# Three blocks instead of two by halves of the weights at the start of a fused attention and two-MLP kernel

## The chip, the cores and the metric

The kernel runs on one core of a Trainium2 chip. The metric is the device time of one execution in microseconds (us), the median of several runs. A profiled execution has its own time, and the span from its first to its last instruction is a little shorter than that.

The core has five engines that run side by side and wait for each other through semaphores: TensorE (PE; its weight loads are listed as PEld), VectorE (DVE), ScalarE (ACT), GpSimd (POOL) and SyncE (SP), which here issues all DMA transfers. The 128-partition on-chip memory is SBUF; matmul results land in PSUM, in eight banks of 128 x 512 f32.

## The reference

Windowed causal attention (window 128, with a linear bias per head), then two MLPs one after the other, on 4 x 576 = 2304 tokens, 8 heads of 64:

```python
scores = scale * np.matmul(q, k.transpose(0, 1, 3, 2))
bias = slopes[:, None, None] * (-np.abs(rel).astype(np.float32))[None, :, :]
mask = (rel >= 0) & (rel < window)
scores = np.where(mask, scores + bias[None], -1000000000.0)
attn = np.exp(scores - np.max(scores, axis=-1, keepdims=True))
attn = attn / (np.sum(attn, axis=-1, keepdims=True) + 1e-09)
x = np.matmul(attn, v)                       # (2304, 512) after the transpose
h = x @ w_in                                 # 512 -> 2048
x = np.where(h >= 1, h, np.where(h <= -1, 0.0, (h + 1) ** 2 / 4)) @ w_out
h2 = x @ w_in2
out = (h2 * np.clip(h2 + 3.0, 0.0, 6.0) / 6.0) @ w_out2
```

The weights arrive as 64-bit floats and are converted on the chip. Products are made from a high and a low part of each factor, three matmuls for one.

## The kernel before, in words

**Attention in ticks.** The tokens are cut into 11 units (lines 72 to 80): 256, 320 | 192, 256, 128 | 256, 128, 192 | 192, 256, 128 tokens. Each unit has 8 heads, each head one step per 128 queries, so the units have 16, 24, 16, 16, 8, 16, 8, 16, 16, 16, 8 steps (`unit_steps`, line 242), 160 in all. `Attention.tick` (lines 513 to 527) is a software pipeline: tick t does stage A (scores, mask, exponential) of step t, stage B (transposes of the probabilities through bank `t`, `th` and `tl` out of it) of step t - 2, and stages C (times v, into bank `r`) and D (into x) of steps three or four back. It also prepares one head ahead (`prep`: the high and low parts of k, q and v) and loads two heads beyond that one. So a unit's x is complete `LAG_D` = 4 ticks after its last step began. Heads of units 0 to 2 are "whole": they normalise after the product with v, stage A issues filler matmuls for them (`keep_busy`, line 345), and v is split only from unit 3 on (line 308). Bank `t` alternates with `t2` up to unit 3 and is alone from unit 4 on (line 373); `s` and `r` are single.

**Weights in 16 pairs.** Pair f holds 128 columns of w_in and 128 rows of w_out. `W1.load` issues one 512 KB DMA; `conv_tick` (lines 199 to 210) converts: two ScalarE passes for pair n, and three VectorE passes, a ScalarE copy and a VectorE subtraction for pair n - 1 (lines 178, 179, 185 to 189, 137, 144).

**The first MLP in blocks and chunks.** `blocks1` cuts the tokens into three blocks of 256 (the x of block j comes from unit j) and four of 384. `chunks.run` does one chunk: `first` for pair f (12 matmuls into bank `h0` or `h1`, line 549; then r, g on VectorE, ScalarE and POOL, lines 578 to 582), then `flush`, the `second` of the pair two chunks back (12 matmuls into the accumulators, line 591). Around it the hook is called twice, between and after; these are the slots. `run_block` runs a block over A (pairs 0 to 7), Z (8 to 15) or FULL. A block run by halves writes its sums to HBM after A (`finish`, line 617); in Z they are read back two chunks before the end (`fetch`, line 604) and added (line 614) instead of copied.

**The order around the change** is written by hand in lines 779 to 788: after 20 ticks ahead of all chunks, `spread(part, ticks, conv)` hands out so many ticks and conversions evenly over the slots of a pass, the ticks over all but the last two slots, and one `W1.load` per slot while there are any. It traces them in this order: block 0 A with 24 ticks and 8 conversion calls, block 1 A with 10 and 4, block 0 Z with 6 and what is left (3), block 1 Z with 4, block 2 FULL with 20, then the blocks of 384. SyncE runs its DMAs in exactly the order written (line 720). The other engines are ordered by the planner, which starts from this order and moves an instruction ahead of another where it expects the other to wait.

The x of all blocks lies in one SBUF tile; block 3's x overwrites that of block 0 and of half of block 1, block 4's that of block 2 and the other half of block 1 (`x_base`, lines 90 to 97).

Of the kernel before, what the change touches and what calls it, by code (L numbers as in the profile page):

```python
# [32 lines left out]
LAG_B, LAG_C, LAG_C_SPLIT, LAG_D = 2, 3, 4, 4  # L33
# [5 lines left out]
def tile_window_attention_two_mlps(  # L39
# [16 lines left out]
    B, H, D, S = qT.shape  # L56
# [3 lines left out]
    KF = DFF // P  # L60
# [9 lines left out]
    blocks1 = [(a, N1) for a in range(0, 3 * N1, N1)] + [(a, WIDE) for a in range(3 * N1, NT, WIDE)]  # L70
# [12 lines left out]
    needs = [min(i + 1 for i, (a, n) in enumerate(units) if a + n >= t0 + m) for t0, m in blocks1]  # L83
    assert needs[:3] == [1, 2, 3]
    first_wide = 3
# [26 lines left out]
    def keep_busy(bank, n):  # L112


        for a in range(0, n, 2 * P):
            nc.tensor.matmul(bank[:, a:a + 2 * P], zeros[:, :P], zeros, start=True, stop=True, skip_group_check=True)

    def make_consts():
        rel = cpool.tile([P, 2, PIECE], F32, tag="m", name="rel")[:, 0, :2 * P]


        nc.gpsimd.iota(rel, pattern=[[1, 2 * P]], base=-P, channel_multiplier=-1,
                       allow_small_or_imprecise_dtypes=True)
        nc.gpsimd.affine_select(out=rel, in_=rel, compare_op=ALU.is_ge, fill=NEG / min(slopes),
                                base=P, pattern=[[-1, 2 * P]], channel_multiplier=1)
        last = nc.gpsimd.affine_select(out=rel, in_=rel, compare_op=ALU.is_ge, fill=NEG / min(slopes),
                                       base=WINDOW - 1 - P, pattern=[[1, 2 * P]], channel_multiplier=-1)
        with tc.issue_after(last.ins):
            make_identity(nc, ident)
        nc.vector.tensor_copy(dist, rel)  # L130
# [93 lines left out]
    heads = []  # L224
# [17 lines left out]
    unit_steps = [sum(1 for n, _ in steps if heads[n].unit == j) for j in range(len(units))]  # L242
# [484 lines left out]
    A, Z = range(KF // 2), range(KF // 2, KF)  # L727

    def run_block(mlp1, j, part, hook):
        for f in part:  # L730
            chunks.run(mlp1, j, f, part, j, lambda: hook(f, 0), lambda: hook(f, 1))

    with ExitStack() as actx:
        mlp1 = Mlp1(W1, blocks1, rpool, gpool)
        raw = actx.enter_context(tc.tile_pool(name="raw", bufs=2))
        proc = actx.enter_context(tc.tile_pool(name="proc", bufs=2))
        work = actx.enter_context(tc.tile_pool(name="work", bufs=2))
        dist = actx.enter_context(tc.tile_pool(name="dist", bufs=1)).tile([P, 2 * P], BF16, tag="dist", name="dist")
        zeros = actx.enter_context(tc.tile_pool(name="zeros", bufs=1)).tile([P, 2 * P], BF16, tag="zeros", name="zeros")
        att = Attention(raw, proc, work, XX)  # L740

        nc.vector.memset(zeros, 0.0)

        nc.scalar.copy(zeros[:, 0:1], nc.const_aps.tensor(0.0, [P, 1], F32))
        bank = psum.tile([P, BANK], F32, tag="h1", name="busy")
        for _ in range(WARM_UP):
            keep_busy(bank, BANK)
        make_consts()
        for vt in att.vts:
            nc.gpsimd.memset(vt[:, :, 0:2 * D + 2:2 * D + 1], 1.0)  # L750
        att.more_loads(1)
        W1.load()

        n_pre = unit_steps[0] + LAG_D
        for t in range(n_pre):
            att.tick()
            if t % 3 == 0:
                W1.load()
            if t >= n_pre - 2:
                W1.conv_tick()  # L760

        def spread(part, ticks, conv):

            slots = 2 * len(part)
            att0, conv0 = att.t, W1.n_conv

            def hook(f, after):
                k = 2 * (f - part[0]) + after + 1
                W1.load()
                while W1.n_conv < conv0 + min(conv, -(-conv * k // slots)) and W1.conv_tick():  # L770
                    pass
                while att.t < att0 + min(ticks, -(-ticks * k // (slots - 2))):
                    att.tick()

            return hook

        run_block(mlp1, 0, A, spread(A, unit_steps[1], KF // 2))
        run_block(mlp1, 1, A, spread(A, 10, KF // 4))  # L780
        run_block(mlp1, 0, Z, spread(Z, unit_steps[2] - 10, KF // 2))
        run_block(mlp1, 1, Z, spread(Z, 4, KF))
        for j in range(2, len(blocks1) - 1):
            if j == first_wide:

                mlp1.tags = ("h0",)
            ticks = sum(unit_steps[:needs[j + 1]]) + LAG_D - att.t
            run_block(mlp1, j, FULL, spread(FULL, max(0, ticks), 0))
# [100 lines left out]
```

## Time and profile before

| | us |
|---|---|
| median of 3 runs | 1000.5 |
| lowest, highest | 999.63, 1001.77 |
| profiled execution | 999.68 |
| its span, first to last instruction | 997.9 |
| PE busy in the span | 968.9 (97%) |
| DVE busy | 602.9 (60%) |
| ACT busy | 515.9 (52%) |
| POOL busy | 259.3 (26%) |

A profile row of a timeline begins with the start and the length in us; `x12` is the number of instructions merged in it, and `[0.81 <-DVE ...]` says how long the engine stood idle before it and what ended the wait. Matmuls are pipelined: the length of one is longer than the distance to the next, so costs of TensorE are read from starts to starts. A window's row gives, for each engine, the busy time and the number of instructions.

### The profile page before, as it was taken

The numbers are of one execution on the slowest core, as the hardware profiler recorded it, in microseconds if no ns is written. First come the engines' busy times: TensorE is split into PE (matmuls) and PEld (weight loads), VectorE is DVE, ScalarE is ACT, GpSimd is POOL, SyncE is SP. The second block draws the span as 40 slices with busy tenths as digits, with TensorE's granted clock in tenths as the row PEclk, the third lists the DMA queues.
The fourth block names the chain that finished last, engine by engine and source line by source line (L and its number), as shares of the span: only waits on it lengthen the run. The fifth ranks groups of instructions, "written<-read, shape, count | busy, mean of one in ns | idle before, by whom it ended". The sixth has DMA issues, their size and how long they took to land.

```text
span 997.9 us, 16828 instructions
## 1 busy us (share of the span) xinstructions
PE 968.9 (97%) x5748; PEld 882.8 (88%) x5748; DVE 602.9 (60%) x1544; ACT 515.9 (52%) x1260; POOL 259.3 (26%) x403
## 2 busy tenths in 40 slices
PE   7799999999999999999999999999999999999998
PEld 5687888999999998899999999999988888888886
DVE  4889996587678666668764998942242224223222
ACT  5688874567657566656653878522242223222121
POOL 3335454456545555455530000000000000000000
PEclk9899999999999999999999999999999999999999
DMA  5685823223212121222203884000030002001001
GB/s 171 168 258 173 271 66 87 78 67 94 75 42 80 50 80 44 63 59 80 62 12 105 293 277 169 1 1 1 1 106 1 1 1 84 1 1 43 1 1 42
DMA packets 75092, 80.00 MB, mean 80 GB/s; under 512 B 8704, under 2 KB 67072, under 8 KB 75008
## 3 DMA queue, kind: packets, MB, share of 16 engines
q1 hardware_dynamic: 75008, 78.94, 25.8%
q8 instruction: 45, 0.74, 0.3%
q14 instruction: 39, 0.32, 0.1%
HBM read 68.42 MB, written 10.49 MB: 79 GB/s over the span
## 4 chain that ended last, share of the span: by engine, by line
PE 85%; DVE 6%; ACT 4%; issue 2%; DMA 2%; POOL 1%; SPq 0%; ACTq 0%; DVEq 0%; POOLq 0%
PE h L549 37%; PE acc L646 20%; PE acc L591 17%; PE s L329 3%; PE r L466 3%; PE r L411 2%; PE t L380 1%; PE t L381 1%; DVE kl L305 1%; DVE r L578 1%; DMA qr<-qT 1%; ACT p L353 1%; DVE r L580 1%; DVE p L350 1%; DMA vr<-v 1%
## 5 line engine op out<-in xcount | busy, mean ns | idle before, releaser
L549 PE MATMUL h<-x,wa 128*128 128x384 f32 (+1 forms) x1344 | 231.5, 316 | 4.4 <-DVE r L580 2.5
L591 PE MATMUL acc<-g,wa 128*128 128x384 f32 (+1 forms) x1344 | 228.8, 315 | 1.7 <-POOL g L144 1.5
L549 PEld LDWEIGHTS h<-x,wa 128*128 128x128 f32 x1344 | 207.6, 190 | 7.0 <-DVE r L580 4.4
L549 PE MATMUL h<-x,wb 128*128 128x512 f32 (+1 forms) x960 | 210.5, 368 | 0.0
L591 PEld LDWEIGHTS acc<-g,wa 128*128 128x128 f32 x1344 | 206.3, 189 | 4.0 <-POOL g L144 2.2
L646 PE MATMUL acc<-wb,g 128*128 128x512 f32 x864 | 209.4, 390 | 0.0
L549 PEld LDWEIGHTS h<-x,wb 128*128 128x128 f32 x960 | 176.3, 188 | 25.0
L646 PEld LDWEIGHTS acc<-wb,g 128*128 128x128 f32 x864 | 161.7, 188 | 32.3
L636 DVE SCALAR_TENSOR_TENSOR r<-r,h 128x512 f32<-128x512 f32 (+1 forms) x80 | 50.7, 633 | 195.5 <-ACT r L635 195.4
L635 ACT ACTIVATE r<-h 128x512 f32<-128x512 f32 (+1 forms) x80 | 44.4, 556 | 207.9 <-PE h L549 207.8
L137 ACT CAST g<-r 128x384 fp32r<-128x384 f32 (+2 forms) x192 | 98.3, 512 | 69.6 <-DVE r L636 48.7
L144 POOL TENSOR_TENSOR g<-r,g 128x256 fp32r<-128x256 f32 (+1 forms) x96 | 92.0, 958 | 129.2 <-ACT g L137 114.0
L579 ACT ACTIVATE r<-r 128x384 f32<-128x384 f32 (+1 forms) x112 | 53.6, 478 | 93.5 <-DVE r L578 93.3
L353 ACT ACTIVATE p<-p,sm 128x256 f32<-128x256 f32 (+2 forms) x160 | 76.0, 476 | 24.4 <-DVE sm L350 21.6
L144 DVE TENSOR_TENSOR g<-r,g 128x384 fp32r<-128x384 f32 (+1 forms) x96 | 59.9, 624 | 44.7 <-ACT g L137 44.6
L578 DVE TENSOR_SCALAR r<-h 128x384 f32<-128x384 f32 (+1 forms) x112 | 55.5, 496 | 37.4 <-PE h L549 33.2
L144 POOL TENSOR_TENSOR qs<-qr,qs 64x256 fp32r<-64x256 f32 (+3 forms) x88 | 68.8, 781 | 28.4 <-issue 7.5
L580 DVE TENSOR_TENSOR r<-h,r 128x384 f32<-128x384 f32 (+1 forms) x112 | 55.7, 497 | 28.9 <-ACT r L579 28.3
L350 DVE CUSTOM_DVE_ANT_0 p<-s,dist 128x256 f32<-128x256 f32 (+2 forms) x160 | 59.7, 375 | 11.1 <-PE s L329 8.8
L358 POOL TENSOR_SCALAR p<-p,sm 128x256 f32<-128x256 f32 (+1 forms) x104 | 48.1, 463 | 61.7 <-DVE sm L357 37.4
L329 PE MATMUL s<-kh,qs 128*128 128x256 f32 (+2 forms) x160 | 55.0, 347 | 1.8 <-POOL qs L144 1.2
L305 DVE SCALAR_TENSOR_TENSOR kl<-kr,kh 128x256 fp32r<-128x256 f32 (+4 forms) x88 | 51.7, 587 | 7.3 <-ACT kh L303 7.1
(75 smaller groups left out, 1153.5 us busy)
## 6 DMA issues: line engine op xcount, KB each, us to landing
rawa<-w_in SPq DMA_DIRECT2D x16, 512.0 KB, 5.6
rawa<-w_out SPq DMA_DIRECT2D x16, 512.0 KB, 5.1
rawb<-w_in SPq DMA_DIRECT2D x16, 512.0 KB, 3.8
rawb<-w_out SPq DMA_DIRECT2D x16, 512.0 KB, 4.6
kr<-kT SPq DMA_DIRECT2D x80, 64.0 KB, 2.3
out<-o SPq DMA_DIRECT2D x18, 256.0 KB, 2.1
qr<-qT SPq DMA_DIRECT2D x64, 64.0 KB, 2.3
vr<-v SPq DMA_DIRECT2D x24, 128.0 KB, 2.4
```

What stands on the lines that cost most here:

```text
L137: nc.scalar.copy(hi, x)
L144: engines[eng].tensor_tensor(out=lo, in0=x, in1=hi.bitcast(F32), op=ALU.subtract)
L305: nc.vector.scalar_tensor_tensor(out=u.kl[:, :nk], in0=u.kr[:, :nk], scalar=unit, in1=u.kh[:, :nk].bitcast(F32), op0=ALU.mult, op1=ALU.sub ...
L329: nc.tensor.matmul(ps[:m, :nk], q[:, qo:qo + m], k[:, ko:ko + nk], start=(w == 0), stop=(w == len(parts) - 1))
L350: nc.vector.tensor_tensor_reduce(out=pt[:m, :nk], in0=ps[:m, :nk], in1=dist[:m, bo:bo + nk], scale=-slopes[u.h], scalar=3.0e38, op0=ALU.ad ...
L353: nc.scalar.activation(out=pt[:m, :nk], in_=pt[:m, :nk], func=AF.Exp, bias=sm[:m, 0:1], scale=-1.0, accum_out=None if u.whole else sm[:m, ...
L549: nc.tensor.matmul(ps[:, :n], self.W.w_in(a, c, f), self.x_chunk(x, b, c, n), start=(k == 0), stop=(k == 3 * KC - 1))
L578: nc.vector.tensor_scalar(out=r[:, :n], in0=ps[:, :n], scalar1=-1.0, scalar2=1.0, op0=ALU.max, op1=ALU.min)
L579: nc.scalar.activation(out=r[:, :n], in_=r[:, :n], func=AF.Square, bias=0.5, scale=0.5)
L580: nc.vector.tensor_tensor(out=r[:, :n], in0=ps[:, :n], in1=r[:, :n], op=ALU.max)
L591: nc.tensor.matmul(acc[i][:, o * n:(o + 1) * n], self.W.w_out(a, f)[:, e * P:(e + 1) * P], g[:, b, :n], start=(first and k == 0 and o == 0 ...
L646: nc.tensor.matmul(acc[t][:, :DM], g[:, b, t * P:(t + 1) * P], self.W.w_out(a, f), start=(first and k == 0), stop=(last and k == 2))
```

## The change

The third block (block 2) joins the first two: its pass over the first half of the weights comes right after block 1's, and its pass over the second half after block 1's. For that, the attention of unit 2 has to be complete before the end of block 1's first pass, so that pass gets 16 ticks instead of 10. The conversions of the second half of the weights are spread over block 1 A (2 calls), block 2 A (3) and the first chunk of block 0 Z (the last 2). The remaining 24 ticks up to block 3, all of units 3 and later, are handed out 3, 8 and 13 to block 0 Z, block 1 Z and block 2 Z; the bounds 3 and 11 are where stage D begins to overwrite x that block 0, then block 1, still needs. Block 2 gets one more `finish` and one `fetch`. The number of matmuls, ticks, loads and conversions is unchanged.

```diff
+        t_end = sum(unit_steps[:3]) + LAG_D
+        per_chunk = 2 * len(heads[H * first_wide].qbs)
+        assert LAG_D == LAG_C_SPLIT and per_chunk == 4
         run_block(mlp1, 0, A, spread(A, unit_steps[1], KF // 2))
-        run_block(mlp1, 1, A, spread(A, 10, KF // 4))
-        run_block(mlp1, 0, Z, spread(Z, unit_steps[2] - 10, KF // 2))
-        run_block(mlp1, 1, Z, spread(Z, 4, KF))
-        for j in range(2, len(blocks1) - 1):
+        run_block(mlp1, 1, A, spread(A, t_end - att.t, KF // 8))
+        run_block(mlp1, 2, A, spread(A, 0, 3))
+        run_block(mlp1, 0, Z, spread(Z, per_chunk - 1, KF))
+        run_block(mlp1, 1, Z, spread(Z, 2 * per_chunk, 0))
+        assert att.t == t_end + 3 * per_chunk - 1
+        run_block(mlp1, 2, Z, spread(Z, sum(unit_steps[:needs[3]]) + LAG_D - att.t, 0))
+        for j in range(first_wide, len(blocks1) - 1):
```

## Rows read from the trace of the kernel before

**Rows 1.** The page, part 1: busy us, share of the span, instructions.
```profile
PE 968.9 (97%) x5748; PEld 882.8 (88%) x5748; DVE 602.9 (60%) x1544; ACT 515.9 (52%) x1260; POOL 259.3 (26%) x403
```

**Rows 2.** Windows by pass (A0, A1, Z0, Z1, B2): stretch, length, busy us of each engine.
```profile
29.24:98.33 69.09, 61.28 (x448) 52.28 (x446) 63.33 (x153) 56.16 (x129) 29.83 (x30) 0.98 0.66 198
98.33:135.40 37.07, 36.35 (x281) 32.37 (x280) 34.23 (x85) 31.38 (x74) 18.21 (x21) 1.00 0.64 206
135.40:167.77 32.37, 30.43 (x239) 27.93 (x238) 26.84 (x70) 19.09 (x53) 16.90 (x20) 1.00 0.35 101
167.77:193.86 26.09, 26.09 (x223) 26.09 (x221) 15.40 (x46) 12.61 (x35) 10.76 (x16) 1.00 0.24 74
193.86:257.90 64.04, 63.38 (x534) 62.37 (x532) 50.52 (x180) 44.45 (x144) 35.81 (x63) 1.00 0.27 71
```

**Rows 3.** Timeline of PE in Z1: start, length, instructions.
```profile
179.37 1.60 PE L591 MATMUL acc<-g,wa 128*128 128x256 f32 x12
180.81 0.22 PE L466 MATMUL r<-th,vs 128*128 128x128 f32 x1
...
181.46 1.61 PE L549 MATMUL h<-x,wa 128*128 128x256 f32 x12
```

**Rows 4.** Timeline of PE at the start of Z0, a tick of a whole head.
```profile
135.40 1.60 PE L549 MATMUL h<-x,wa 128*128 128x256 f32 x12
136.93 0.58 PE L411 MATMUL r<-vr,th 128*64 128x65 f32 x4
...
137.89 0.33 PE L591 MATMUL acc<-g,wa 128*128 128x256 f32 x1
```

**Rows 5.** Groups by shape: count, busy us, mean ns, idle before; conversion, x, add.
```profile
L189 DVE CUSTOM_DVE_ANT_0 ma<-rawa,ma 128x2048 uint16<-128x2048 uint16 x16 | 21.5, 1341 | 0.7 <-ACT rawa L179 0.6
...
L144 DVE TENSOR_TENSOR wa<-ma,wa 128x1024 fp32r<-128x1024 f32 x16 | 20.9, 1304 | 0.9 <-ACT wa L137 0.8
L187 DVE SCALAR_TENSOR_TENSOR ma<-rawa,ma 128x1024 uint32<-128x1024 uint32 x16 | 20.8, 1297 | 0.1
...
L185 DVE TENSOR_SCALAR ma<-ma 128x1024 uint32<-128x1024 uint32 x16 | 12.5, 780 | 0.9 <-ACT ma L178 0.8
...
L144 DVE TENSOR_TENSOR x<-xf,x 128x192 fp32r<-128x192 f32 x8 | 3.6, 446 | 0.0
...
L614 DVE TENSOR_TENSOR o<-acc,o 128x512 f32<-128x512 f32 x4 | 2.7, 686 | 0.2 <-PE acc L591 0.2
```

**Rows 6.** Waits of PE, 98 to 170 us: us in total, times, longest; first and last of five.
```profile
PE h L549 <- DVE sm L356: 0.8, 1, 0.8
...
PE t L381 <- ACT th L137: 0.2, 1, 0.2
```

**Rows 7.** Timeline in Z0 where unit 3's v is waited for: ScalarE and TensorE.
```profile
157.91 0.35 ACT L141 CAST vs<-vr 128x192 fp32r<-128x192 f32 x1 [1.32 <-DMA vr<-v]
...
159.65 1.57 PE L591 MATMUL acc<-g,wa 128*128 128x256 f32 x11 [0.64 <-POOL g L144]
```

**Rows 8.** Window in B2 that holds the eight ticks of unit 4.
```profile
219.60:244.40 24.80, 24.78 (x209) 24.25 (x208) 20.33 (x75) 18.46 (x61) 14.77 (x29) 1.00 0.34 86
```

**Rows 9.** Timelines of DVE, POOL and PE around a wait for bank `t` in block 4.
```profile
367.63 1.15 DVE L144 TENSOR_TENSOR x<-xf,x 128x192 fp32r<-128x192 f32 x1
368.70 0.21 DVE L393 TENSOR_TENSOR tl<-t,th 64x64 fp32r<-64x64 f32 x1
...
367.36 1.20 POOL L144 TENSOR_TENSOR g<-r,g 128x384 fp32r<-128x384 f32 x1 [0.46 <-ACT g L137]
...
369.06 0.30 PE L380 MATMUL t<-ident,p 128*128 128x128 f32 x1 [1.08 <-DVE sm L356]
```

**Rows 10.** Waits of PE for transposes in block 4, 342 to 448 us.
```profile
PE t L380 <- DVE sm L356: 2.4, 3, 1.1
PE t L381 <- DVE sm L356: 2.4, 4, 0.8
```

**Rows 11.** Tile kr, loads between 100 and 117 us, from issue to landing.
```profile
DMA to landing us min/median/max: 2.0/8.3/9.0
```

## The prediction

> **What bounds the kernel now.** I read the page first. TensorE is busy for 97% of the span [rows 1], so the change can only give back time in which TensorE waits, or lose some. Next I cut the part that the change touches into its stages, each beginning with the first matmul of a block's pass. I call the passes A0, A1 (first half of the weights, blocks 0 and 1), Z0, Z1 (second half) and B2 (block 2, all weights). Their windows are [rows 2]. Everything before 98.33 us (the end of A0) is traced identically in both kernels, and so is everything from block 3 on (257.90 us). What is in question is the 159.57 us between.
>
> Pure MLP time there: a group of twelve 256-column matmuls takes 1.44 us when nothing interrupts it (179.37 to 180.81) [rows 3], so a chunk (one `first`, one `second`) takes 2.88 and eight chunks 23.04. The five passes hold 40 chunks, 115.2 us. The other 44.4 us belong to 40 attention ticks, each with its own matmuls, and to waits. By stage, the surplus per tick, from the windows [rows 2] and the tick counts of the code, is: A1 14.03 us for 10 ticks, Z0 9.33 for 6 (together 1.46 each); Z1 3.05 for 4 (0.76); B2 17.96 for 20 (0.90). A tick in a saturated stretch of Z1 takes 0.65 (180.81 to 181.46) [rows 3]. A tick of the first kind (units 0 to 2, with a filler matmul) took 1.05 where no wait stands in it (from 136.84, which is 135.40 plus 1.44, to 137.89) [rows 4]. So A1 and Z0 run about 0.4 us a tick over that, some 6.5 us in all; Z1 runs without loss.
>
> The reason is VectorE: busy 92% of A0, 92% of A1, 83% of Z0, then 59% of Z1 and 79% of B2 [rows 2]. A weight conversion costs it 0.78 + 1.30 + 1.34 + 1.30 = 4.7 us [rows 5]. In A1 and Z0 together TensorE's named waits are five, 2.5 us [rows 6]; one chain of them is not VectorE's: unit 3's v arrives late, ScalarE stands 1.32 us for it, and the second matmul group behind it waits for POOL's `g` [rows 7].
>
> **The change, part by part.** The same 40 chunks, 40 ticks and 7 conversion calls are laid out over A1, A2, Z0, Z1, Z2. Ticks: 16, 0, 3, 8, 13 (before: 10, 6, 4, 20). Conversion calls: 2, 3, 2, 0, 0 (before 4, 3, 0, 0).
>
> A1, 16 ticks, 2 conversions. VectorE loses 9.4 us of conversions and gains six ticks. With the waits of [rows 6] taken off, ticks cost (23.36 - 2.5)/16 = 1.30: 23.04 + 20.9 = 43.9 us. Ends: 1.05 a tick, 39.8; as before, 1.46, 46.4. I take the middle, since the wait for v [rows 7] moves here with its tick and since a head's q and k now follow each other faster.
>
> A2, no tick, 3 conversions. Z1's VectorE time less four ticks at 1.9 (below) is 7.8 us for eight chunks; with 14.2 of conversions 22.0 of 23.04 by the means, which overlap. I add 0.5: 23.5 (23.0 to 25.0). Its first `first` needs unit 2's x, finished by the last tick one chunk earlier; that chunk's 2.88 us are the cover.
>
> Z0, 3 ticks, and both remaining conversions traced in its first chunk: 23.04 + 3 x 0.76 = 25.3. The 9.4 us of VectorE queue ahead of the next chunks' clamps. Two chunks' time (5.76) hides most; uncovered it is 3.6 (28.9). I take 0.5: 25.8, as the weights are due only six chunks later.
>
> Z1, 8 ticks: 23.04 + 8 x 0.76 = 29.1; at B2's 0.90, 30.2. I take 29.4.
>
> Z2, 13 ticks in 14 slots, where B2 had 20 in 30. At 0.90 a tick: 34.7. But each half chunk now carries a tick: TensorE needs 1.44 + 0.90 = 2.34 us for the pair. VectorE, in the stretch of unit 4's eight ticks, was busy 20.33 of 24.80 us [rows 8], which hold (24.8 - 7.2)/2.88 = 6.1 chunks; at 0.84 to 1.0 a chunk, 1.8 to 1.9 is left per tick. With half a chunk that is 2.3 of 2.34 us: VectorE becomes as scarce as TensorE. The banks `t`, `s` and `r` are single in unit 4, so TensorE cannot run ahead. The nearest rows of such waits are in block 4, with about one tick in 3.3 us: 4.8 us for transposes [rows 10] over 32 ticks, 0.15 each. At a denser pace I take 0.2, 2.6 us: 37.3. Ends: nothing, 34.7; every second tick waiting like the longest one (1.08) [rows 9], 7.0, 41.7.
>
> One more block boundary: block 2's first half is written out, read back, and added instead of copied. That is two adds of 0.69 on VectorE [rows 5] in place of one copy each on ScalarE and VectorE, and four DMAs of 256 KB. The read is issued two chunks ahead; I cost it at nothing. If SyncE is held by a k or q load ahead of it, the price is that load's wait, and `finish` stalls VectorE.
>
> SyncE runs in written order, so the weight loads (one a slot, eight left, all in A1) are interleaved with more q, k and v loads; see the third rival. The adds of Z1 and Z0 queue ahead of the clamps of the next pass, in Z2 at its densest; that is in the 0.2.
>
> **Sum.** 43.9 + 23.5 + 25.8 + 29.4 + 37.3 = 159.9, against 159.57: +0.3 us. Added to the profiled run (999.68) that is 1000.0; the median of the three runs is 0.8 higher, so 1000.8 by it. I write 1000.5. All low ends give 151.9, all high ends 172.2, but they are not independent: the same work is only moved.
>
> **The rivals.**
> *The early gain stays.* TensorE leads in A1 again and ticks cost 1.15 (41.4); A2 23.2, Z0 25.4, Z1 29.2, Z2 with 1.2 of waits 35.9. Sum 155.1, 4.5 us less: 996. For it: Z1 at 59% has no loss at all [rows 2]; A1's VectorE share falls to some 72% ((34.2 - 9.4 + 6 x 0.9) / 42), and the loads become more even (92, 83, 59, 79% before). Against: Z2's 2.3 of 2.34.
>
> *Z2 is VectorE's.* In Z2 the transposes of tick t wait until VectorE has emptied `t` of tick t - 1, and VectorE has no spare slot to catch up in, as it has now after every second tick. The rows show how it goes: x's low part takes 1.15 us, `tl` behind it ends at 368.91, TensorE starts at 369.06 after standing idle for 1.08 [rows 9]. At 0.45 a tick Z2 costs 40.6, the whole 3.3 us more than the forecast: 1004. It decides from the point where a tick and half a chunk take VectorE more than 2.34 us. In the rows that `x` subtraction took 1.15 us beside a POOL subtraction of 1.20 that began 0.27 earlier [rows 9], while its mean is 0.45 [rows 5]. The Trainium skill's page "SBUF — State Buffer", "Who interferes with whom", says that a VectorE instruction with two SBUF inputs and a GpSimd instruction that reads SBUF block each other entirely, the later one waiting; the trace agrees here. By that rule the denser Z2, where POOL's work per microsecond rises too, gets VectorE times above the means I used: at 0.70 more in every second of the 13 ticks 4.6 us, some 1005 in place of 1000.5, so it speaks against the change and for this rival.
>
> *Late q and k.* In A1 the k loads beside weight loads landed after 2.0 to 9.0 us, median 8.3 [rows 11]. A head now passes every 2 x 2.74 = 5.5 us instead of 7.4 or more; two heads' lead is 11 us, less the issue and the preparation. If three heads come 1 us late, +3: 1003.5.
>
> *The change does little.* All queues but SyncE's are ordered by the planner. If it puts Z2's ticks off into block 3's slots, the order is much as before: within 1 us.
>
> **Chances.** Forecast 0.35, no effect through the planner 0.05, early gain 0.33, Z2 on VectorE 0.19, late q and k 0.08. About 0.2% (2 us) is what a measurement can tell from no change. So faster 0.33, same 0.40, slower 0.27. Forecasts within no change run from 998.5 to 1002.5; the range takes in both rivals with a little beyond, 995.5 to 1005, and leaves out the far ends of A1 and Z2.
>
> **What will show it.** Cut by the first matmuls of passes, A1 should last 42 to 45 us, A2 23 to 24 with no wait over 0.5, Z0 under 26.5, Z1 29 to 30, Z2 36 to 39 with VectorE above 88% and waits of transposes or `r` matmuls. Block 3 should begin within 2 us of 257.9. The wait of ScalarE for `vr` should appear near A1's end. The forecast is wrong if Z2 runs under 35.5 (ticks then fit in VectorE's holes) or above 40, if A1 shows waits for `kr` or `qr`, or if the time after block 3's start differs by more than 1 us from before.

## The result, and the profile after

The changed kernel takes 1007.97 us (median of 5 runs, 1005.47 to 1011.28) where the kernel before takes 1000.1 (5 runs, 999.11 to 1001.77). The ratio is 1.0077, with a 95% interval of 1.0052 to 1.0103: slower by 0.8%. The prediction said 1000.5, with a range of 995.5 to 1005.0 and 0.27 for slower. The time lies above the range.

Times of one kernel scatter with the mean granted clock of the run: in one series the kernel before took 999.99 us at 0.995 and 1006.34 at 0.986. Three executions, one of e14 (1332.76 us) and two of e8 (3277.4 and 2289.48), lie far above the others and are left out of the ratios and of the fit. Where runs are compared closely below, all other runs of the kernels in the table went into one fit, with a level for each kernel and a common slope against the clock lost, (0.995 - mean granted clock) x 1000 us. The slope is 0.70 us per us. "At the same clock" is the difference of two levels: the changed kernel is 6.1 us slower than the one before (95%: 5.0 to 7.1).

The page of the changed kernel, part 1, which answers [rows 1]:

```profile
PE 974.8 (97%) x5748; PEld 886.7 (88%) x5748; DVE 601.7 (60%) x1539; ACT 518.1 (51%) x1267; POOL 257.3 (26%) x403
```

The same matmuls take 5.9 us more of a span that is 8.2 us longer (1006.1 in place of 997.9). The other engines are busy as before. The windows of the passes, which answer [rows 2]; stretch, length, busy us of PE, PEld, DVE, ACT, POOL, then the granted clock, share and rate of DMA. The rows are A0, A1, A2, Z0, Z1, Z2:

```profile
30.20:99.10 68.90, 62.50 (x448) 53.38 (x447) 62.28 (x154) 56.29 (x129) 29.45 (x29) 0.95 0.66 197
99.10:144.00 44.90, 42.93 (x319) 37.00 (x318) 38.67 (x111) 35.12 (x92) 20.40 (x27) 0.99 0.64 199
144.00:170.00 26.00, 25.73 (x202) 25.15 (x201) 21.31 (x41) 15.62 (x35) 10.91 (x14) 0.94 0.20 57
170.00:195.10 25.10, 25.10 (x213) 25.10 (x212) 12.83 (x36) 11.29 (x32) 9.76 (x13) 1.00 0.20 64
195.10:225.00 29.90, 29.78 (x250) 29.31 (x250) 22.22 (x72) 18.71 (x55) 15.31 (x24) 1.00 0.23 64
225.00:266.60 41.60, 36.38 (x293) 34.56 (x293) 32.31 (x116) 29.34 (x101) 23.13 (x43) 1.00 0.38 103
```

From first matmul to first matmul the passes last:

| pass | forecast (ends) | measured | difference |
|---|---|---|---|
| A1 | 43.9 (39.8 to 46.4) | 44.9 | +1.0 |
| A2 | 23.5 (23 to 25) | 26.0 | +2.5 |
| Z0 | 25.8 (25.3 to 28.9) | 25.0 | -0.8 |
| Z1 | 29.4 (29.1 to 30.2) | 29.9 | +0.5 |
| Z2 | 37.3 (34.7 to 41.7) | 41.6 | +4.3 |
| sum | 159.9 | 167.4 | +7.5 |

Before, the same work took 159.57 us: 69.4 for A1 and Z0, which held the 16 early ticks and the conversions, and 90.1 for Z1 and B2 with the other 24 ticks. Now the early ticks and the conversions stand in A1 and A2, 70.9 us, and the 24 ticks in Z0 to Z2, 96.5. What follows block 3's first matmul takes 739.5 us (266.58 to 1006.1), and took 740.0 before. A0 begins and ends 0.75 to 1.0 us later, with a granted clock of 0.95 in place of 0.98. So the time was lost in A1 to Z2, most of it in Z2. Against the forecast, Z2 is 4.3 us over, and A1 and A2 together 3.5.

**Z2.** Its waits of PE, from 225.0 to 266.6 (us in total, times, longest):

```profile
PE t L380 <- POOL p L358: 2.9, 1, 2.9
...
```

The longest wait, followed back through four timelines of the changed kernel, first that of PE:

```profile
240.29 0.33 PE L380 MATMUL t<-ident,p 128*128 128x128 f32 x1 [2.92 <-POOL p L358]
```

POOL:

```profile
238.93 0.46 POOL L144 TENSOR_TENSOR qs<-qr,qs 64x128 fp32r<-64x128 f32 x1 [2.78 <-ACT qs L137]
239.48 1.21 POOL L358 TENSOR_SCALAR p<-p,sm 128x256 f32<-128x256 f32 x2
```

VectorE, the last step that this `p` needs ahead of POOL:

```profile
236.60 0.15 DVE L357 RECIPROCAL sm<-sm 128x1 f32<-128x1 f32 x1
```

ScalarE:

```profile
238.55 0.30 ACT L137 CAST qs<-qr 128x128 fp32r<-128x128 f32 x1 [2.01 <-DMA qr<-qT]
238.76 0.50 ACT L353 ACTIVATE p<-p,sm 128x256 f32<-128x256 f32 x1
```

The transposes wait for `p` of their head, the first of the two on POOL. Its reciprocal was ready at 236.75, but on POOL it stands behind the `qs` of a later head, which waits for its cast on ScalarE. The cast waits 2.01 us for a load of q. On ScalarE the exponential of the next `p` stands behind the cast in the same way. So a late load for one head holds up the probabilities of others, because ScalarE and POOL work in order. The issue of that load, at 234.46, is on the timeline of SyncE's queue (`x2` is a pair of loads):

```profile
234.46 1.18 SPq L263 DMA_DIRECT2D qr<-qT  x2
235.68 1.89 SPq L270 DMA_DIRECT2D vr<-v  x1
237.68 0.93 SPq L617 DMA_DIRECT2D x2d<-o  x2
238.71 1.11 SPq L263 DMA_DIRECT2D kr<-kT  x2
239.91 1.21 SPq L263 DMA_DIRECT2D qr<-qT  x2
241.22 1.18 SPq L263 DMA_DIRECT2D kr<-kT  x2
242.50 1.19 SPq L263 DMA_DIRECT2D qr<-qT  x2
243.80 0.51 SPq L270 DMA_DIRECT2D vr<-v  x1
244.42 1.28 SPq L263 DMA_DIRECT2D kr<-kT  x2
```

That load was also slow to land. Its time from issue to landing, tile `qr` between 234.4 and 235.6:

```profile
DMA to landing us min/median/max: 3.4/3.6/3.8
```

The median of q's loads in Z2 is 2.2; with it the load would have been there some 1.2 us earlier (an estimate from these numbers). Why it landed late is not shown. But it is one load of many, and the queue had no slack: from one row to the next SyncE stands idle for 0.12 us at most. Two heads with their v, without anything between, take 244.42 - 238.71 = 5.71 us, 2.86 a head. In Z2 a tick of unit 4 is a whole head and there is one per half chunk; the forecast counted 2.34 us for it. The queue can't follow, and it can't work ahead either: from 223.93 to 230.69 it stood for a free buffer of k, as the waits of SyncE's queue in Z2 show:

```profile
SPq L263 <- DVE kl L305: 6.7, 1, 6.7
...
```

The kernel before shows the same price, in the stretch of [rows 8]:

```profile
220.01 1.11 SPq L263 DMA_DIRECT2D kr<-kT  x2
...
225.10 0.59 SPq L270 DMA_DIRECT2D vr<-v  x1
225.78 1.10 SPq L263 DMA_DIRECT2D kr<-kT  x2
```

That is 5.77 us for two heads, while TensorE gave a head 3.1 us there (eight in 24.8). SyncE was just fast enough: ScalarE waited for one load in that stretch.

```profile
ACT qs L137 <- DMA qr<-qT: 0.5, 1, 0.5
...
```

In Z2 of the changed kernel it waits for six:

```profile
ACT qs L137 <- DMA qr<-qT: 2.9, 4, 2.0
...
ACT kh L303 <- DMA kr<-kT: 0.8, 2, 0.4
```

**The end of A1 and A2.** Timeline of PE just ahead of the first matmul of A2, at 144.01:

```profile
141.75 0.39 PE L329 MATMUL s<-kh,qs 128*128 128x256 f32 x1 [0.54 <-POOL qs L144]
143.18 0.33 PE L380 MATMUL t<-ident,p 128*128 128x128 f32 x1 [1.04 <-POOL p L358]
```

Then the granted clock falls to 0.50, the 1.2 GHz level, for 3.4 us, and the matmuls of A1's last ticks (two transposes, scores, `x`, `r`) stand in A2 still. The window of that stretch; from its end to that of A2 the clock is 1.00:

```profile
143.55:146.95 3.40, 3.40 (x18) 3.09 (x16) 1.23 (x4) 1.86 (x6) 2.83 (x5) 0.50 0.22 59
```

### The profile page after: what moved, and what is told of

It reads as the page before. It is cut to its first block, busy times and chain, and to the rows that moved or that the text cites. A ratio compares the mean times of both kernels' runs of the same rounds, so it can differ in the third digit from the quotient of the medians.

```text
span 1006.1 us, 16862 instructions
## 1 busy us (share of the span) xinstructions
PE 974.8 (97%) x5748; PEld 886.7 (88%) x5748; DVE 601.7 (60%) x1539; ACT 518.1 (51%) x1267; POOL 257.3 (26%) x403
## 4 chain that ended last, share of the span: by engine, by line
PE 84%; DVE 5%; ACT 4%; DMA 2%; issue 2%; POOL 2%; SPq 1%; POOLq 0%; ACTq 0%; DVEq 0%
PE h L549 37%; PE acc L646 20%; PE acc L591 17%; PE s L329 2%; PE r L466 2%; PE r L411 2%; PE t L380 2%; PE t L381 1%; DMA qr<-qT 1%; DMA vr<-v 1%; SPq L263 1%; DVE kl L305 1%; ACT p L353 1%; DVE p L350 1%; PE busy L116 1%
## 5 line engine op out<-in xcount | busy, mean ns | idle before, releaser
L549 PE MATMUL h<-x,wa 128*128 128x384 f32 (+1 forms) x1344 | 234.2, 318 | 2.4 <-DVE r L580 1.3
L549 PEld LDWEIGHTS h<-x,wa 128*128 128x128 f32 x1344 | 209.7, 191 | 5.2 <-DVE r L580 2.2
L646 PEld LDWEIGHTS acc<-wb,g 128*128 128x128 f32 x864 | 161.8, 188 | 32.3
L353 ACT ACTIVATE p<-p,sm 128x256 f32<-128x256 f32 (+2 forms) x160 | 76.2, 477 | 26.3 <-DVE sm L350 23.0
L144 DVE TENSOR_TENSOR g<-r,g 128x384 fp32r<-128x384 f32 (+1 forms) x96 | 60.0, 625 | 45.9 <-ACT g L137 45.7
L144 POOL TENSOR_TENSOR qs<-qr,qs 64x256 fp32r<-64x256 f32 (+3 forms) x88 | 65.9, 749 | 31.7 <-ACT qs L137 9.0
L580 DVE TENSOR_TENSOR r<-h,r 128x384 f32<-128x384 f32 (+1 forms) x112 | 55.7, 497 | 29.4 <-ACT r L579 28.9
```

The source lines that it names most:

```text
L144: engines[eng].tensor_tensor(out=lo, in0=x, in1=hi.bitcast(F32), op=ALU.subtract)
L353: nc.scalar.activation(out=pt[:m, :nk], in_=pt[:m, :nk], func=AF.Exp, bias=sm[:m, 0:1], scale=-1.0, accum_out=None if u.whole else sm[:m, ...
L549: nc.tensor.matmul(ps[:, :n], self.W.w_in(a, c, f), self.x_chunk(x, b, c, n), start=(k == 0), stop=(k == 3 * KC - 1))
L580: nc.vector.tensor_tensor(out=r[:, :n], in0=ps[:, :n], in1=r[:, :n], op=ALU.max)
L646: nc.tensor.matmul(acc[t][:, :DM], g[:, b, t * P:(t + 1) * P], self.W.w_out(a, f), start=(first and k == 0), stop=(last and k == 2))
```

## The experiments

All times are medians; "same clock" is the difference to the kernel before by the fit above, with its 95% bounds. Each ratio is against runs of the kernel before on the same chip (their medians lie between 1000.1 and 1001.5 us); the ratios are those on record, not quotients of the medians shown. Passes are in us, from first matmul to first matmul; B2 of the old order is given as its two halves.

| kernel | us | ratio (95%) | same clock | A1 | A2 | Z0 | Z1 | Z2 (or B2) |
|---|---|---|---|---|---|---|---|---|
| before | 1000.1 | 1 | 0 | 37.1 | | 32.4 | 26.1 | 32.3 + 31.8 |
| after | 1007.97 | 1.0077 (1.0052 to 1.0103) | +6.1 ± 1.1 | 44.9 | 26.0 | 25.0 | 29.9 | 41.6 |
| e3 | 1006.27 | 1.0045 (1.0023 to 1.0068) | +4.4 ± 0.7 | 37.1 | | 32.4 | 26.1 | 28.3 + 41.5 |
| e4 | 1007.59 | 1.0073 (1.0046 to 1.0100) | +5.8 ± 1.0 | 42.8 | | 37.2 | 29.0 | 28.7 + 28.1 |
| e1 | 1006.31 | 1.0051 (1.0023 to 1.0078) | +4.3 ± 0.7 | 45.3 | 23.1 | 25.2 | 29.9 | 38.9 |
| e2 | 1003.16 | 1.0014 (0.9996 to 1.0031) | +0.1 ± 0.7 | 35.8 | | 31.9 | 26.1 | 32.2 + 32.0 |
| e6 | 1007.38 | 1.0059 (1.0032 to 1.0086) | +6.0 ± 0.7 | 44.8 | 25.1 | 25.0 | 29.9 | 41.6 |
| e5 | 1008.63 | 1.0067 (1.0038 to 1.0097) | +5.1 ± 0.9 | 46.0 | 23.1 | 25.2 | 29.9 | 38.1 |
| e14 | 1005.47 | 1.0035 (1.0010 to 1.0061) | +4.3 ± 0.7 | 45.9 | 23.1 | 25.2 | 29.9 | 38.6 |
| e9 | 1007.39 | 1.0054 (1.0026 to 1.0081) | +3.9 ± 0.7 | 45.8 | 23.1 | 25.2 | 29.9 | 39.1 |
| e8 | 1007.23 | 1.0058 (1.0033 to 1.0083) | +6.0 ± 0.8 | 43.5 | 27.0 | 25.0 | 29.9 | 41.3 |
| e10 | 1002.89 | 1.0033 (1.0009 to 1.0057) | +2.0 ± 0.7 | 44.7 | 27.4 | 29.4 | 30.5 | 31.9 |
| e11 | 1004.35 | 1.0053 (1.0034 to 1.0072) | +3.4 ± 1.0 | 46.6 | 23.1 | 29.5 | 30.6 | 31.9 |
| e12 | 1001.75 | 1.0024 (1.0010 to 1.0038) | +1.7 ± 0.7 | 44.7 | 25.1 | 27.5 | 32.5 | 31.9 |
| e13 | 1004.38 | 1.0038 (1.0013 to 1.0062) | +2.5 ± 0.9 | 44.8 | 26.2 | 29.3 | 34.7 | 28.1 |
| e15 | 1002.92 | 1.0000 (0.9980 to 1.0020) | +1.5 ± 0.7 | 44.9 | 26.3 | 27.5 | 32.4 | 31.5 |

e10 to e13 and e15 are for timing only. They hand out more than 3 ticks in Z0 and more than 11 up to the end of Z1, so unit 3's x overwrites part of the x that the last chunks of block 0 and of block 1 still read, and those chunks are computed from it. Instructions and their number are those of the changed kernel.

### The two halves of the change alone

**e3, the dense half alone.** The order before, but block 2's 20 ticks are dealt out as 7 in its first eight chunks and 13 in its last eight, the density of Z2, with no third block by halves.

```diff
-        for j in range(2, len(blocks1) - 1):
...
+                    made[half] = spread(Z, then, 0) if half else spread(A, first, 0)
...
+        run_block(mlp1, 2, FULL, dense(7, 13))
+        for j in range(first_wide, len(blocks1) - 1):
```

> The kernel before with only the density of the last ticks changed: block 2 keeps one pass over all weights, but 7 of its 20 ticks go to its first eight chunks and 13 to its last eight, as in Z2 of the changed kernel. If the pace of the last 13 ticks is the cause (theory S or V), block 2 takes 64.0 + 3 to 5 us and the whole is 1003-1005. If the third block's split itself (one more write, read and add, two passes) or the early part costs the time, this kernel is at 1000 +-1.

Measured: 41.5 us for the dense half, as in Z2, and 28.3 for the thin one: together 69.8, where the kernel before has 64.0. The time is 4.4 us above it at the same clock. The longest group of waits of PE in the dense half:

```profile
PE r L466 <- DVE xf L484: 3.9, 6, 0.9
...
```

It follows that density alone costs what Z2 costs. The extra write and read of block 2's sums, and the adds of Z1 beside Z2, aren't needed for it. The waits sit elsewhere (at `r`, not at one `p`), but the pass is as long. ScalarE waits for loads of k and q here too, 1.5 us each.

**e4, the early half alone.** The order before with 16 ticks in block 1 A; what is left goes to block 0 Z (3), block 1 Z (8) and block 2 FULL (13 in 30 slots).

```diff
-        run_block(mlp1, 1, A, spread(A, 10, KF // 4))
-        run_block(mlp1, 0, Z, spread(Z, unit_steps[2] - 10, KF // 2))
-        run_block(mlp1, 1, Z, spread(Z, 4, KF))
+        run_block(mlp1, 1, A, spread(A, 16, KF // 4))
+        run_block(mlp1, 0, Z, spread(Z, 3, KF // 2))
+        run_block(mlp1, 1, Z, spread(Z, 8, KF))
```

> The kernel before with only the early ticks moved: 16 ticks in A1 (4 conversions there, as before), then 3 in Z0, 8 in Z1 and 13 over the 30 slots of block 2 in one pass. If the end of A1 (v of unit 3 late, then the lower clock) costs 2 to 4 us in the changed kernel, it shows here too: 1002-1003. If the loss is Z2's alone, this kernel is at 999-1000.5, as block 2 has a third fewer ticks.

Measured: +5.8 us at the same clock, and not in A1: Z0 grew to 37.2 us with only 3 ticks, at a granted clock of 0.95. B2 with 13 thin ticks fell to 56.8. The longest wait of PE in Z0 (148 to 186):

```profile
PE h L549 <- DVE r L580: 2.8, 1, 2.8
...
```

Timelines in Z0, of POOL:

```profile
166.75 2.86 POOL L144 TENSOR_TENSOR g<-r,g 128x256 fp32r<-128x256 f32 x1 [0.88 <-ACT g L137]
```

and of VectorE:

```profile
166.67 1.20 DVE L144 TENSOR_TENSOR wa<-ma,wa 128x1024 fp32r<-128x1024 f32 x1
167.80 1.21 DVE L187 SCALAR_TENSOR_TENSOR ma<-rawa,ma 128x1024 uint32<-128x1024 uint32 x1
168.94 0.41 DVE L393 TENSOR_TENSOR tl<-t,th 128x256 fp32r<-128x256 f32 x1
```

Here conversions stand one behind the other on VectorE, ahead of the clamps. They are three in this pass, as in the kernel before, but the last one's line 187 starts 19.7 us into the pass in place of 14.8. A `g` on POOL that takes 0.74 us elsewhere takes 2.86 beside them: it ends at 169.61, when the three VectorE instructions are through. This test doesn't give the price of the early half within the changed kernel, since it makes a new collision.

### The loads

**e1, one load each.** The changed kernel with q and k laid out twice by the host, so that each needs one DMA of 128 partitions in place of two of 64. **e2** is the kernel before with the same edit.

```diff
...
-                for r in range(2):
-                    nc.sync.dma_start(out=dst[r * D:(r + 1) * D, :m], in_=src[u.b, u.h, :, a:a + m])
+                nc.sync.dma_start(out=dst[:, :m], in_=src[u.b, u.h, :, a:a + m])
...
-        "qT": np.ascontiguousarray(q.transpose(0, 1, 3, 2)),
...
+        "qT": np.concatenate([q.transpose(0, 1, 3, 2)] * 2, axis=2),
...
```

> The changed kernel, but each head's q and k come with one DMA instead of two (the arrays are laid out twice along the head dimension beforehand, so one transfer fills both halves of the partitions). A head then costs SyncE 2 to 3 DMA issues instead of 4 to 6, at about 0.59 us each. Theory S (SyncE: in Z2 a head of unit 4 passes every 2.34 us while its loads cost SyncE some 2.7 us, so q lands late and everything behind it stands): the 3.1 us wait at 237 us goes, Z2 shrinks from 41.6 to 36.5-38 us, the whole from 1008 to 1003-1004. Theory V (VectorE and the single banks t, r, s, as the prediction had it): Z2 stays at 40-41.5, the whole at 1006.5-1008. Neither touches the wait at the end of A1 and the clock's fall after it.

> The kernel before with the same single loads of q and k. Theory S: block 2 has its unit-4 heads every 3.25 us on the mean, more than the 2.7 us of SyncE, so little is gained there, 0 to 1 us; the early stages, where q is also waited for, may gain 1 to 3 us: 997-1000. Theory V: no difference, 999.5-1000.5.

Measured: e2 is level with the kernel before (+0.1 ± 0.7). In e1, Z2 falls by 2.7 us to 38.9 and A2 by 2.9 to 23.1; at the same clock it stands 1.8 ± 1.3 us below the changed kernel. Z2 lies between what the two theories expected (36.5 to 38, and 40 to 41.5). SyncE's timeline in Z2 now has gaps (0.92 us behind the v load, from 240.50 to 241.42), and one load takes 0.33 to 0.42 us to issue:

```profile
237.81 0.34 SPq L263 DMA_DIRECT2D kr<-kT  x1
238.25 0.39 SPq L263 DMA_DIRECT2D qr<-qT  x1
...
240.12 0.38 SPq L270 DMA_DIRECT2D vr<-v  x1
241.42 0.33 SPq L263 DMA_DIRECT2D kr<-kT  x1
```

ScalarE waits for no load in Z2 any more. The longest group of waits of PE there is:

```profile
PE r L466 <- DVE xf L484: 1.3, 4, 0.5
...
```

So SyncE's issue is a cause, of 2.7 us in Z2 and some 2 us (+6.1 to +4.3) in the whole. The landing of the loads hardly changed with the edit (median of q 2.0 us in place of 2.2). It isn't all: at 0.90 us a tick Z2 would be 34.7, and it is 38.9. And A1 to Z2 together fell by 5.0 us (162.4 in place of 167.4), the whole by 1.8; where the rest went isn't shown.

### What holds the rest of Z2

**e6 and e5, two banks for `r`.** In unit 4 the tile `r` alternates between its bank and `t2`; e6 is this alone, e5 has e1's single loads as well.

```diff
-                u.r = psum.tile([P, BANK], F32, tag="r", name=f"r{n}")
+                u.r = psum.tile([P, BANK], F32, tag=("r", "t2")[u.h % 2] if u.unit == first_wide + 1 else "r", name=f"r{n}")
```

> The changed kernel with nothing but the second bank for r of unit 4; q and k keep their two loads each. If SyncE's issue of the loads is the root of Z2's 41.6 us: 40.5 to 41.6, with the waits for qr and kr still on ScalarE and the time within 1 us of the changed kernel's. If the bank is the root: 39 or less, 2.5 us or more off the time. If both cost by themselves, the steps add: e1's 2.7 us and this kernel's make up e5's.

> The changed kernel with q and k laid out twice by the host, so that each is one load, and with the tile r of unit 4 in turn in two PSUM banks (its own and t2). Theory: what is left of the loss in Z2 after the loads is the wait for the single bank r (1.3 us in four waits and the pace that they set): Z2 falls from the 38.9 us of e1 to 36 to 37, the waits of r on `xf` are gone, and the time is about 2 us over the kernel before at the same granted clock. Rival, VectorE is simply full in Z2: another bank changes nothing, Z2 stays within 0.5 of 38.9 and the waits turn up as waits for `tl` or for clamps.

Measured: Z2 of e6 is 41.6, as without the edit; Z2 of e5 is 38.1, 0.8 below e1 where 2 to 3 were expected. The waits for `r` go, but for 0.5 and 0.2 us, and those for the other single bank, `t`, come. The longest group of waits of PE in Z2 of e6, and then of e5:

```profile
PE t L380 <- DVE tl L393: 2.6, 2, 2.2
...
```

```profile
PE t L380 <- DVE tl L393: 1.0, 2, 0.5
...
```

**e14, two banks for `t`.** As e1, and the tile `t` of unit 4 alternates with `t2`.

```diff
-            bank = psum.tile([P, BANK], F32, tag=("t", "t2")[(n * 3 + i) % 2] if u.unit <= first_wide else "t",
+            bank = psum.tile([P, BANK], F32, tag=("t", "t2")[(n * 3 + i) % 2] if u.unit <= first_wide + 1 else "t",
```

> As e1 (the changed kernel, q and k loaded once), with the tile t of unit 4 in turn in two banks, as the units before it have it; r keeps its single one. If the bank t holds the heads: Z2 falls from 38.9 to 37 or less, waits for `tl` are gone. If the heads' own chain through ScalarE and VectorE is what is slow, Z2 stays within 0.7 of 38.9 and the waits are for `p` and for `xf`.

Measured: 38.6, 0.3 below e1. Now the waits are those for `r` again:

```profile
PE r L466 <- DVE xf L484: 1.3, 3, 0.6
...
```

Neither bank alone is what holds the heads. There is only one bank to lend, so both together weren't tried.

**e9, less on VectorE.** As e5, with the low part of x of units 3 and 4 made on POOL.

```diff
...
-                self.to_x(u, u.xf, LO["x"])
+                self.to_x(u, u.xf, "pool" if u.unit in (3, 4) else LO["x"])
```

> As e5, with the subtraction that makes the low part of x moved from VectorE to POOL for units 3 and 4. If VectorE is full in Z2, this takes 0.45 to 1.15 us a tick from it: Z2 35 to 36, and the time may come to that of the kernel before or 1 us below. Rival: POOL, with its own subtractions, then sets the pace or holds the port that VectorE's subtractions want: Z2 38 or more, no gain over e5, and in Z1 (unit 3's eight ticks) a loss of up to 1 us.

Measured: 39.1, 1.0 above e5, as the rival had it. The window of Z2 shows 29.31 us of VectorE in place of e5's 31.36, and 26.66 of POOL:

```profile
228.44:267.56 39.12, 35.52 (x294) 34.33 (x293) 29.31 (x109) 29.17 (x101) 26.66 (x49) 1.00 0.37 104
```

VectorE is busy for 75% of the pass and Z2 isn't shorter. Yet this test doesn't take VectorE out of question. The subtractions that left it took 4.1 us in e5, and its busy time fell by 2.05 only, since another of its subtractions became slower. The low part of k, in Z2 of e5 and then of e9:

```profile
L305 DVE SCALAR_TENSOR_TENSOR kl<-kr,kh 128x256 fp32r<-128x256 f32 x11 | 4.9, 446 | 0.0
L305 DVE SCALAR_TENSOR_TENSOR kl<-kr,kh 128x256 fp32r<-128x256 f32 x11 | 6.6, 596 | 0.5 <-ACT kh L303 0.4
```

ScalarE also waits 1.2 us for a load of q here, and for none in Z2 of e5. So e9 shows that this exchange doesn't help; whether less work on VectorE would, without more on POOL, isn't shown.

### The wait for v

**e8.** The changed kernel without the v loads of unit 3's first two pairs of heads; their products are made with what the buffer held.

```diff
             if u.h % 2 == 0:
+                if u.unit == first_wide and u.h < 4:
+                    return
```

> The changed kernel without the v loads of unit 3's first two pairs: v of the buffer's last contents is used, so the output of those heads is another one. Theory: the wait for v at the end of A1 costs some 1.5 us in the pass, and what it brings on, the lower clock at the start of A2, another 1.7: A1 falls from 44.9 to 43.3, A2 from 26.0 to 24, the rest unchanged. Rival, the ticks of A1 cost this without v too (another wait takes its place): A1 44.5 or more, and A2 is short only if the clock stays up.

Measured: A1 falls by 1.4 us, but A2 grows by 1.0 to 27.0, at a granted clock of 1.00: A1 and A2 together are 70.5 where the changed kernel has 70.9. The transposes of the last ticks, and their wait for `p` (0.74 us here, 1.04 in the changed kernel), moved across the border into A2, and another wait, of 0.6, came with them. At the same clock the whole is +6.0, as with v. So a late v isn't what costs the time. On the clock this test decides nothing: it stayed up, as the theory said, but it did so in e6 and e12 too, which load v.

### The ticks spread out

**e10 and its kin.** The changed kernel with other numbers of ticks in Z0, Z1 and Z2 (3, 8, 13 in the change): 7, 8, 9 in e10; the same with e1's single loads in e11; 5, 10, 9 in e12; 7, 11, 6 in e13; e12 with two banks for `t` in e15.

```diff
-        run_block(mlp1, 0, Z, spread(Z, per_chunk - 1, KF))
-        run_block(mlp1, 1, Z, spread(Z, 2 * per_chunk, 0))
...
+        run_block(mlp1, 0, Z, spread(Z, 7, KF))
+        run_block(mlp1, 1, Z, spread(Z, 8, 0))
...
```

> The changed kernel with the ticks of Z0, Z1 and Z2 set at 7, 8 and 9 in place of 3, 8 and 13, nothing else. Theory: the loss stands in Z2 because there a whole head passes with each tick, one every half chunk, faster than SyncE issues its loads (2.7 us a head) and than the single banks turn round; with 9 ticks in 16 slots a head has 3.5 us. Then Z2 costs 23.04 + 9 x 0.9 to 1.0 = 31.2 to 32, Z0 23.04 + 7 x 0.75 to 0.9 = 28.3 to 29.3, Z1 about 30: the three together 90 to 91 where the changed kernel has 96.5, and the time comes to 1001 to 1002. Rival, the ticks cost what they cost wherever they stand (VectorE has as much to do): Z0 grows by more than Z2 falls less 3, the three stay above 94, and the time is 1005 or more.

> As e10, with q and k laid out twice by the host and loaded once. If SyncE's issue is no longer short at this pace, the loads add nothing: Z2 within 0.5 us of e10's, A1 and A2 together 68.4 (as in e1) where the changed kernel has 70.9, and the time 1 to 2 us under e10's. If SyncE still binds at 9 ticks, Z2 is 1 us or more under e10's.

> As e10, with 5, 10 and 9 ticks: Z0, with its two conversions, gets fewer, Z1 without conversions more, so that unit 4's first heads pass in Z1 at nearly a tick per slot. If density is what costs, Z1 at 10 in 16 slots is past the easy pace in its last slots: 32 to 33, Z0 27, Z2 31.5, sum 90.5 to 91.5, the same as e10. If conversions are what costs, e12 is 1 us or more better than e10.

> As e10, with 7, 11 and 6 ticks: three more of unit 4's ticks are moved from Z2 to Z1. By density Z1 then is as Z2 of the changed kernel in its last half (34 to 35), and Z2 falls to 28.5: the sum is 91 to 92, up to 1 us worse than e10. If Z2's cost was its place beside the adds of block 2's first half, and not its density, then Z1 stays at 0.86 a tick (32.5) and the sum is 89.5 or less.

> As e12 (5, 10 and 9 ticks), with the tile t of unit 4 in turn in two banks. At that pace a tick of unit 4 costs 0.98 us in Z2 and 0.95 in Z1, where 0.86 to 0.9 is the price without loss: with the bank as the reason 1.0 to 1.5 us are to be had in both together, and the time comes within 1 us of the kernel before's. Otherwise it is e12's within 0.5 us.

Measured: Z2 with 9 ticks is 31.9 us in e10, e11 and e12 alike, as expected; a tick there costs (31.9 - 23.04) / 9 = 0.98. Z0, Z1 and Z2 together are 91.8 in e10, 92.0 in e11, 91.9 in e12 and 92.1 in e13, where the changed kernel has 96.5 and e1 94.0; that is 0.1 to 0.8 more than was expected of e10, e12 and e13. At the same clock, e10 gives back 4.1 us and e12 4.4 of the 6.1. Windows of Z1 and Z2 in e12:

```profile
196.29:228.75 32.46, 31.85 (x265) 30.94 (x264) 25.42 (x87) 21.48 (x67) 17.43 (x29) 1.00 0.26 67
228.75:260.62 31.87, 31.33 (x265) 30.93 (x264) 24.34 (x89) 22.63 (x77) 19.27 (x34) 1.00 0.42 121
```

The longest wait of PE in the two:

```profile
PE h L549 <- DVE x L144: 0.3, 1, 0.3
...
```

Not a load is waited for on TensorE or ScalarE, and no wait of TensorE is over 0.3 us. VectorE's share of Z2 is 76%, as it was 78% with 13 ticks: the mean share doesn't tell the two passes apart, the density does. e13 puts 11 ticks into Z1, which then takes 34.7 (1.06 a tick), and Z2 with 6 takes 28.1 (0.84): the price of a tick goes with the density of its pass, not with Z2's place. The three passes together lose next to nothing by it (92.1 against 91.8). So 11 ticks in a pass still cost little more than 9, and the step to 13, at 1.43 a tick here and 1.42 in e3, is the dear one.

e11 missed on two of its numbers. A1 and A2 together were 69.7, not 68.4, and its time is above e10's, not below: Z2 is no shorter, so the single loads bring it nothing where the heads come every 3.5 us. Before A1 the five kernels with single loads differ by up to 6 us, with other stretches of lower clock in each, so what they cost there can't be read. e15 gains 0.5 us in Z1 and Z2 over e12 (1.0 to 1.5 expected) and 0.2 at the same clock: the bank `t` isn't it at this pace either. Its ratio tells it from neither the kernel before nor e12.

As the note under the table says, none of these orders can stand as it is: the bounds 3 and 11 belong to the place of x in SBUF. With that place, the changed order forces 13 ticks into Z2. A version that beats the kernel before wasn't found.

## Why the prediction was wrong

**What bounds the kernel, and what the change touches.** Right. TensorE is the bound, the loss is in A1 to Z2, and from block 3 on nothing changed (739.5 against 740.0).

**Z0 and Z1.** Right within 0.8 and 0.5 us: ticks cost 0.65 and 0.86 us there. The two conversions that the forecast put into Z0's first chunk didn't run in Z0 at all (see A1 and A2), so the 0.5 us for them had nothing to pay for.

**Z2, the step that failed.** "At a denser pace I take 0.2, 2.6 us: 37.3." The waits cost 6.9 over the 34.7, not 2.6. The far end of the step, 41.7, held the 41.6, but the range left it out. Two things in the reasoning were wrong:

- SyncE's issue was put at nothing. Loads were weighed only in a rival, for A1, and at the block boundary the text had "If SyncE is held by a k or q load ahead of it" and no sum. The sum was there to be made in the trace of before: 5.77 us of issue for two heads, 2.9 a head, against the 2.34 that the forecast itself had worked out for a tick and half a chunk. Over eight heads, at the 2.86 of Z2, that is 4.2 us of issue that can't be done in the time (an estimate from these numbers), and e1 gets 2.7 of Z2 back.
- The rest was put down to VectorE, "as scarce as TensorE", with a share above 88% as its sign. The share was 78%, in part because the pass is longer: the same 32.31 us would be 93% of 34.7. e9 doesn't settle it, since another instruction of VectorE became slower there. Single loads, another bank for `r` or for `t`, and 2 us less on VectorE with more on POOL leave Z2 between 38.1 and 39.1. What removes the loss is only the pace: 0.98 a tick at 9 ticks against 1.22 (e1) and 1.43 at 13. That a head's chain through ScalarE, VectorE and POOL, each in order, is then too long for the single banks is argued from the waits that move from bank to bank. It isn't shown, and the 3.4 us between e5's 38.1 and 34.7 (2.5 of them idle time of TensorE) stay without a single named cause.

**The rival "Z2 is VectorE's"** had the right pass, sign and nearly the price (40.6; measured 41.6). For the 2.7 us that e1 gives back it had the wrong engine; for the rest VectorE is neither shown nor excluded. It had 0.19. The Trainium skill's page "SBUF — State Buffer", section "Who interferes with whom", was weighed for it: a VectorE instruction with two SBUF inputs and a GpSimd instruction that reads SBUF shut each other out. The trace agrees, but the price is small: of the low parts of x, those of 128x128 take 600 ns in Z2 and took 450 in B2, while those of 128x256 take 797 and took 761. The groups of 128x128, by shape, in B2 of the kernel before and in Z2 of the changed one:

```profile
L144 DVE TENSOR_TENSOR x<-xf,x 128x128 fp32r<-128x128 f32 x4 | 1.8, 450 | 0.0
L144 DVE TENSOR_TENSOR x<-xf,x 128x128 fp32r<-128x128 f32 x4 | 2.4, 600 | 0.0
```

That is 0.7 us of VectorE in the pass, where the rival had 4.6 by this rule. e9, with these on POOL, is no faster, but there `kl` takes 596 ns in place of 446, so the contention seems to have moved, not gone.

**A1 and A2.** They took 70.9 us together; 67.4 were forecast, and the same ticks and conversions took 69.4 before. The first step that failed is "VectorE loses 9.4 us of conversions". Line 187 has one instruction for each conversion. Its windows in A1 of the kernel before, and then in A1, A2 and Z0 of the changed one (length, busy us, count):

```profile
98.33:135.40 37.07, 4.84 (x4) 1.00 0.64 206
99.10:144.00 44.90, 4.92 (x4) 0.99 0.64 199
144.00:170.00 26.00, 4.29 (x3) 0.94 0.20 57
170.00:195.10 25.10, 0.00 (x0) 1.00 0.20 64
```

Traced were 2, 3 and 2 in these passes; 4, 3 and none ran there. In A1 and in A2 the planner ran two conversions ahead of their place, so VectorE lost none in A1 and was busy for 86% of it (38.67 of 44.90 us). The other step that failed is "With the waits of [rows 6] taken off": the 16 ticks that cost 23.4 us over the chunks before cost 24.8 now, 23.7 in e12 where the clock stays up in A2, and 22.4 in e1. The old waits went and others came, 0.5 and 1.0 us at the end of A1, with part of the last ticks' work running into A2. How much of the 3.5 us over the forecast belongs to the conversions isn't shown. "The early gain stays" was wrong too: there is no early gain to see, as e1's 22.4 stand against 21.6 in e2, the old order with the same loads. The lower clock at A2's start had no place in the forecast; it costs about 1 us (26.0 against 25.1 in e6 and e12, which have the same waits and a clock of 1.00). The cause was looked for in v (e8), which decides nothing on it; that A2 has no tail with single loads (23.1 in all five kernels) speaks for the loads of q and k, but A1 is longer by 0.4 to 1.7 us in these, and ScalarE waits for no load in A1 of the changed kernel. It stays open.

**The size of what remains.** e12, without the density, is 1.7 ± 0.7 us over the kernel before at the same clock; its A1 to Z2 sum to 161.7, 2.1 over 159.6. Of that, 0.4 us are in A1 and A2 (69.8 against 69.4) and 1.7 in the 24 ticks of Z0 to Z2 (91.9 against 90.1; 0.95 a tick against 0.88). So about 4.4 of the 6.1 us go with the 13 ticks in Z2. The other 1.7 lie mostly in the later ticks, too.

**The signs that were named.** "The forecast is wrong if Z2 runs ... above 40" came true, and block 3 began at 266.58, not within 2 us of 257.9. Of the others, a wait for `vr` near A1's end wasn't there, A2 wasn't under 24, and VectorE wasn't above 88%. Z0, Z1 and the time after block 3's start were as said.

## What to carry to other kernels

When work is moved closer together, make one sum for every queue that each item passes through, the one that only issues transfers included: its time per item, read back to back from the timeline, against the new distance between items. An engine that is just in time in the old profile shows next to no wait (0.5 us for one load here), and can be the first to be late in the new one; mean busy shares don't tell. And where an order has bounds from the place of data (here x that is overwritten), look first at which stretch those bounds push the work into.

## What the runs showed of the hardware

- Two loads of 64 partitions take SyncE 1.1 to 1.2 us to issue, one of 128 partitions, as many bytes, 0.33 to 0.42 (e1). To issue the same bytes as one DMA costs about a third here.
- At the median landing didn't change: loads of q land 2.2 us after issue in Z2 (3.8 at most), and 2.3 (3.3) in the stretch of [rows 8]. The 3.8 belongs to the load behind the longest wait of TensorE.
- The same two waits at the end of A1 (0.5 and 1.0 us) were followed by a granted clock of 0.50 for 3.4 us in the changed kernel, e13 and e15, for 6.8 in e10, and by none in e6 and e12. So the order of the instructions alone doesn't settle whether the clock falls, and A2 cost 25.1, 26.0 to 26.3, or 27.4 us.
- A POOL subtraction of 0.74 us took 2.86 beside conversions on VectorE (e4). A VectorE subtraction of 446 ns (e5) took 596 at the mean where others had been moved from VectorE to POOL (e9).
